# A recurrent attention layer with two expert layers on one core: group 1's triangular inverse computed by halves on GpSimd, and three changes of order

## The chip, the cores and the metric

The kernel runs on one core of a Trainium2 chip. The metric is the device time of one execution in microseconds, as the median of several runs. The core has five engines that work at the same time, each with a queue of its own that it works off in order: TensorE (PE in the rows), VectorE (DVE), ScalarE (ACT), GpSimd (POOL) and SyncE (SP), which here issues all transfers.

## The reference, cut to what matters

```python
B, H, S, D = 4, 8, 768, 48
k_n = k / (norm(k) + 1e-6)
for t in range(S):                       # per batch and head: a state of 48 x 48
    y[t] = q[t] @ state
    v_old = state.T @ k_n[t]
    state = state + beta[t] * outer(k_n[t], v[t] - v_old)
x = y as 3072 rows of 384
g = x @ w_gate                           # 384 -> 1536
x = (g * sigmoid(g) * (x @ w_val)) @ w_out       # 1536 -> 384
h = x @ w_in                             # 384 -> 2048
out = where(h > 0, h, exp(min(h, 0)) - 1) @ w_out2   # 2048 -> 384
```

All numbers are float32.

## The kernel before, in words

The 3072 tokens are cut into 12 groups of 256 (two batches, 128 time steps, all 8 heads: 16 pairs of head and batch). Inside a group the recurrence over time is computed in four chunks of 32 steps. Within a chunk the recurrence becomes a triangular system, so each group needs the inverse of a unit triangular 32 x 32 matrix for each of its 64 chunks; all of them lie side by side on the 128 partitions.

A group goes through these steps. `norms` computes the lengths of the rows of k. `prepare` transposes k and q on TensorE (L698), multiplies them with each other into small Gram matrices (L748), masks and scales these on VectorE (L758, L768), and calls `invert`. `invert` transposes the Gram matrices (L852), eliminates row by row with pairs of a product (L869, L885) and a sum (L876, L891), and transposes the result back (L900). For a group in `BLOCKED` it eliminates only the two diagonal halves of 16 rows, both in one instruction (15 pairs, `halves`), and builds the off-diagonal half by two joins on TensorE (L917, L933) with a turn (L910) and a middle step (L924) on VectorE between them and a copy on ScalarE (L937) at the end. In the kernel before that is so for group 0 alone, on VectorE; groups 1 to 11 eliminate all 32 rows on GpSimd (31 pairs, `whole`). Then `attention` applies the inverse (the X step, L994), forms the chunks' matrices (L1031, evacuated at L1050 and L1052), chains the states (L1081, L1090), reads out y (L1121) and transposes it (L1164) into the two float32r parts, high (L1174) and low (L1179), of the MoE input, in tile xa or xb.

The first MoE layer (`moe1`) runs for single groups 0 to 3 with 256 columns, and for pairs (4 and 5, and so on) with 512. Each of its 16 steps has two projections (L1350, nine matmuls each) and an output product (L1382, nine). The second layer (`moe2`) follows at the end for pairs. The first layer's weights are 24 tiles of two halves, loaded at L1228 and split by `decode` into a high and a low part: two steps on ScalarE and a copy (L1264, L1270, L1284), two steps on VectorE (L1274, L1288). All 24 stay in SBUF.

The order of the work is not that of the code. Every step is added to a planner (`Order`) with a priority, its inputs and outputs and an expected duration on its engine; `Order.run` then places the steps one after the other and so writes each engine's queue. The table `SLOW` stretches the expected durations of an inverse on GpSimd. Where the plan has TensorE idle before the first MoE matmul it puts in matmuls without use (L1551, L1557). Priorities of attention are `att_pri(g)` and a little more; group 1's preparation and attention have 14.7 (`P1`), group 2's preparation 25.

Group 1 has a tile of its own for its inverse before: `own`, which lies in the place of weight 22 (`LATE`). That weight's transfer therefore waits for group 1's X step, and group 0's second evacuation tile lies in the places of weights 21 and 23 (`LC0`). Group 1's masks are separate ones for the two Gram matrices (L758). A weight half waits for the one two before it (`PACE`). Groups 4 to 11 run the X step as two halves; groups 1 to 3 as one joint step.

Of the kernel before, what the change touches and what calls it, by code (L numbers as in the profile page):

```python
# [22 lines left out]
class Step:  # L23
    __slots__ = ("big", "shy", "alts", "pri", "succ", "np", "ready", "need", "use", "by")

    def __init__(self, alts, pri):
        self.alts = alts
        self.pri = pri
        self.succ = []
        self.np = 0  # L30
        self.ready = 0.0
        self.need = ()
        self.use = ()
        self.by = None
        self.shy = None
        self.big = False
# [15 lines left out]
class Order:  # L52
# [9 lines left out]
    SEED = 0  # L62
    SPREAD = 0.0
    FROM = 14.0
# [8 lines left out]
    def __init__(self):  # L73
        self.rng = Random(self.SEED)
# [90 lines left out]
    def link(self, b, o):  # L165
        b.succ.append(o)
        o.np += 1

    def run(self, until):
# [22 lines left out]
        while left:  # L192
# [113 lines left out]
def delta_moe_kernel(ctx: ExitStack, tc: tile.TileContext, q, k, v, beta,  # L306
# [31 lines left out]
    BIG = ()  # L338
# [324 lines left out]
    def prepare(g, p):  # L663
# [67 lines left out]
        joint = g >= 2  # L731
        if not two:
            both = [Slots([GV[x]] if g == 1 else AT, 1) for x in range(2)]
        for a in range(2):
            if not joint:
                l = []
            for par in range(2):
# [14 lines left out]
                def mask(k0, k1, a=a, par=par, h=h, w0=w0):  # L752
# [3 lines left out]
                    if g == 1 and k0 == 0 and a == 0 and par == 0:  # L756
                        buf['m1'] = TT(hm.got[0], [128, 16, 32])
                    V.tensor_tensor(out=buf['m1'][:, us].unsqueeze(2) if g == 1 and k0 == 0 else  # L758
                                    win(gr[:, a * 8 + par:a * 8 + par + 1, o:o + 1],
# [13 lines left out]
                def rest(a=a, par=par, h=h, mask=mask, masks=masks):  # L773
# [6 lines left out]
                    if g == 1:  # L780
                        one = a == 0 and par == 0
                        add(p, dvp(128, lambda: mask(0, 1)), r=[(h, a)] + zk + ([] if one else ["m1"]),
                            w=[("m1", a, par)] + (["m1"] if one else []), use=[h] if one else [h, hm],
                            need=[hm] if one else [])
                        add(p + 0.15, dvp(128, lambda: mask(1, 2)), r=[(h, a)] + zk,
                            w=[("grq", 1, a, par)] + GX[1][a], use=[h])
                        return
                    if not two:
                        add(p, dvp(256, lambda: mask(0, 2)), r=[(h, a) if g == 1 else h] + zk,
                            w=[("grm", a, par), ("grq", g % 2, a, par)] + (GX[1][a] if g == 1 else []),  # L790
                            use=[h])
                        return
# [7 lines left out]
            if not joint:  # L800
                batch(p, 6, l, g > 0, need=(both if a == 0 else []) if g == 1 else None)
                if g == 1:
                    def later_(a=a):
                        x = gr[:, a * 8:a * 8 + 8, 32 + 80 * (g % 2):64 + 80 * (g % 2)]
                        G.tensor_tensor(out=x, in0=x, in1=strict.unsqueeze(1).to_broadcast([128, 8, 32]), op=ALU.mult)
                    add(p + 0.2, pool(256, later_), r=["strict"], w=[("grq", g % 2, a, 0), ("grq", g % 2, a, 1)])
# [7 lines left out]
        invert(g, p, later, hm)  # L814
# [872 lines left out]
```

## Time and profile before

| | |
|---|---|
| median of 3 runs | 1104.2 us (1103.76 to 1109.05) |
| profiled execution, own time | 1101.52 us |
| its span, first to last instruction | 1099.8 us |
| TensorE busy | 1073.1 us, 98% of the span |
| VectorE, ScalarE, GpSimd busy | 607.1, 536.9, 347.4 us |
| mean granted TensorE clock | 0.988 of full speed |
| transfers | 57.07 MB, mean 52 GB/s |

A row of a timeline gives the start in us from the span's beginning, the duration, the engine, the line of the kernel, the operation, the tiles written and read, the number of instructions merged into the row, and in brackets how long the engine stood idle before it and whose event ended that. A row of windows gives a stretch, the busy time of an engine in it, and the clock granted to TensorE, where 1.00 is 2.4 GHz and 0.50 is 1.2 GHz.

### The profile page before, as it was taken

How to read it: one execution, taken by the hardware profiler on the slowest of the kernel's cores; microseconds unless marked ns; L12 is line 12 of the kernel's file. 1: busy time of each engine (PE TensorE's matmuls, PEld its weight loads, DVE VectorE, ACT ScalarE, POOL GpSimd, SP SyncE). 2: the span in 40 equal slices, each digit the busy share in tenths (PEclk: the TensorE clock that was granted, in tenths of full speed). 3: DMA queues.
4: the chain of work that ended last, by engine and by line, in shares of the span. 5: the costliest groups of instructions: out<-in, count | busy, mean ns of one | idle time of the engine just before them, and what ended most of it. 6: DMA issues, size and time to landing. Idle time of an engine off the chain costs nothing.

```text
span 1099.8 us, 29926 instructions
## 1 busy us (share of the span) xinstructions
PE 1073.1 (98%) x12848; PEld 931.3 (85%) x12848; DVE 607.1 (55%) x1182; ACT 536.9 (49%) x1072; POOL 347.4 (32%) x765
## 2 busy tenths in 40 slices
PE   7899899999999999999999999999999999999998
PEld 6589799999988887888777788888888888898887
DVE  7988666666345644564434466545345454444534
ACT  6878444544243424433322577645445454454443
POOL 1788787778730864064720000000000000000000
PEclk9889899999999999999999999999999999999999
DMA  8585032123002201220100456101001010000000
GB/s 168 169 216 134 17 46 46 26 39 60 2 23 43 41 2 38 42 42 16 30 13 1 153 180 205 46 1 48 10 1 58 1 58 1 10 29 1 29 2 29
DMA packets 104949, 57.07 MB, mean 52 GB/s; under 512 B 77392, under 2 KB 97360, under 8 KB 104816
## 3 DMA queue, kind: packets, MB, share of 16 engines
q1 hardware_dynamic: 104816, 55.16, 20.2%
q8 instruction: 100, 1.64, 0.6%
q14 instruction: 33, 0.27, 0.1%
HBM read 45.71 MB, written 9.44 MB: 50 GB/s over the span
## 4 chain that ended last, share of the span: by engine, by line
PE 89%; DVE 4%; POOL 3%; ACT 2%; issue 1%; DVEq 0%; POOLq 0%; ACTq 0%
PE gv L1350 26%; PE acc L1382 10%; PE gv L1476 9%; PE acc L1514 9%; PE at L1476 9%; PE at L1514 9%; PE at L1382 3%; PE at L1031 3%; PE at L1081 3%; POOL ain L869 2%; PE acc L1551 2%; PE at L994 2%; PE at L748 2%; PE at L698 1%; POOL z L876 1%
## 5 line engine op out<-in xcount | busy, mean ns | idle before, releaser
L1350 PE MATMUL gv<-xa,w 128*128 128x512 f32 (+1 forms) x1008 | 220.1, 350 | 1.6 <-DVE hb L1374 0.7
L1350 PEld LDWEIGHTS gv<-xa,w 128*128 128x128 f32 x1008 | 160.4, 190 | 27.2 <-DVE hb L1374 2.4
L1382 PE MATMUL acc<-hb,w 128*128 128x256 f32 (+1 forms) x720 | 153.8, 333 | 0.2 <-ACT hb L1369 0.2
L869 POOL TENSOR_TENSOR ain<-z,ain 128x126 f32<-128x126 f32 (+22 forms) x310 | 125.8, 406 | 57.2 <-DVE ain L852 30.6
L1350 PE MATMUL gv<-xb,w 128*128 128x256 f32 (+1 forms) x720 | 140.6, 329 | 0.0
L876 POOL TENSOR_TENSOR z<-z,ain 128x126 f32<-128x126 f32 (+22 forms) x310 | 122.5, 395 | 23.7
L1361 DVE TENSOR_TENSOR gv<-gv,tb 128x256 f32<-128x256 f32 (+1 forms) x96 | 54.1, 564 | 134.5 <-PE gv L1350 101.0
L1350 PEld LDWEIGHTS gv<-xb,w 128*128 128x128 f32 x720 | 108.6, 191 | 13.1 <-issue 0.2
L1358 ACT ACTIVATE tb<-gv 128x256 f32<-128x256 f32 (+1 forms) x96 | 47.2, 491 | 145.6 <-PE gv L1350 145.4
L1382 PEld LDWEIGHTS acc<-hb,w 128*128 128x128 f32 x720 | 106.5, 190 | 12.7 <-ACT hb L1369 0.4
L1369 ACT CAST hb<-gv 128x256 fp32r<-128x256 f32 (+1 forms) x96 | 46.0, 479 | 113.0 <-DVE gv L1361 112.6
L1491 DVE SCALAR_TENSOR_TENSOR hb<-gv,hb 128x512 f32<-128x512 f32 x45 | 31.1, 691 | 81.4 <-ACT hb L1488 81.4
L1374 DVE TENSOR_TENSOR hb<-gv,hb 128x256 fp32r<-128x256 f32 (+1 forms) x96 | 53.4, 557 | 38.1 <-PE at L1382 23.5
L1482 ACT ACTIVATE hb<-gv 128x512 f32<-128x512 f32 x45 | 26.9, 597 | 79.7 <-PE gv L1476 79.7
L1382 PE MATMUL at<-hb,w 128*128 128x512 f32 x144 | 56.2, 391 | 0.0
L1488 ACT ACTIVATE hb<-hb,zn 128x512 f32<-128x512 f32 x70 | 50.7, 725 | 2.2
L1491 DVE SCALAR_TENSOR_TENSOR hb<-at,hb 128x512 f32<-128x512 f32 x25 | 17.3, 692 | 59.0 <-ACT hb L1488 58.9
L1485 ACT ACTIVATE hb<-hb 128x512 f32<-128x512 f32 x70 | 44.3, 632 | 2.1
L1482 ACT ACTIVATE hb<-at 128x512 f32<-128x512 f32 x25 | 14.9, 597 | 61.9 <-PE at L1476 61.8
L1031 PEld LDWEIGHTS at<-gr,R 32*96 32x96 f32 x1260 | 37.0, 163 | 8.5 <-issue 5.3
L1476 PE MATMUL at<-lc,w 128*128 128x512 f32 x150 | 42.8, 393 | 0.0
L1476 PE MATMUL gv<-R,w 128*128 128x512 f32 x150 | 42.7, 395 | 0.0
(262 smaller groups left out, 2221.5 us busy)
## 6 DMA issues: line engine op xcount, KB each, us to landing
w<-in_moe_w_out_dram SPq DMA_DIRECT2D x28, 384.0 KB, 4.3
w<-in_moe_w_in_dram SPq DMA_DIRECT2D x16, 384.0 KB, 3.9
w<-in_moe_w_gate_dram SPq DMA_DIRECT2D x12, 384.0 KB, 4.2
w<-in_moe_w_val_dram SPq DMA_DIRECT2D x12, 384.0 KB, 4.2
kq<-in_q_dram SPq DMA_DIRECT2D x11, 384.0 KB, 6.4
x2d<-hb SPq DMA_DIRECT2D x16, 256.0 KB, 2.7
kp<-in_k_dram SPq DMA_DIRECT2D x10, 384.0 KB, 4.9
R<-in_v_dram SPq DMA_DIRECT2D x24, 96.0 KB, 2.2
```

The lines of the kernel that those rows point to most:

```text
L869: E.tensor_tensor(out=t, in0=z[:, l:l + 1, x:y].to_broadcast([128, m, y - x]), in1=an[:, l + 1:32, l:l + 1].to_broadcast([128, m, y - x]), ...
L876: E.tensor_tensor(out=z[:, l + 1:32, x:y], in0=z[:, l + 1:32, x:y], in1=t, op=ALU.add)
L1031: PE.matmul(bank[h[c].got[0]][0:96, i:i + 80], lhsT=R[t, u, :], rhs=gr[t, u, o0:o0 + 80], start=True, stop=True, skip_group_check=True)
L1350: PE.matmul(dst, lhsT=wt[:, a_, kk * 128:(kk + 1) * 128], rhs=X[b_][:, :, kk, :] if two else X["one", g][:, b_, kk, :], start=(n == 0), st ...
L1358: A.activation(out=c['s'], in_=gate(0), func=ACTF.Silu)
L1361: V.tensor_tensor(out=gate(1), in0=gate(1), in1=c['s'], op=ALU.mult)
L1374: V.tensor_tensor(out=c['h'][1], in0=gate(1), in1=c['h'][0].bitcast(F32), op=ALU.subtract)
L1382: PE.matmul(sums(d), lhsT=wt[:, a_, d * 128:(d + 1) * 128], rhs=c['h'][b_], start=(f == 0 and n == 0 and (two or d != 1)), stop=(f == F1 - ...
L1476: PE.matmul(x, lhsT=W[f][:, 0, a_, kk * 128:(kk + 1) * 128], rhs=x2[n][b_][:, kk, :], start=(m == 0), stop=(m == 3 * KD - 1))
L1488: A.activation(out=c['r'], in_=c['r'], func=ACTF.Identity, bias=neg1, scale=1.0)
L1491: V.scalar_tensor_tensor(out=c['r'], in0=bank[h.got[0]], scalar=0.0, in1=c['r'], op0=ALU.max, op1=ALU.add)
L1514: PE.matmul(o, lhsT=c['h'][:, b_, t * 128:(t + 1) * 128], rhs=W[f][:, 1][:, a_, :], start=(f == 0 and m == 0), stop=(f == F2 - 1 and m == 2))
```

## The change

Group 1 joins group 0 in `BLOCKED`, but its fifteen pairs run on GpSimd; the joins on TensorE follow as in group 0. It now uses the common tiles `ain` and `z` in place of `own`, so weight 22 waits for no X step and group 0's second evacuation tile lies in the places of weights 22 and 23. Group 1's four Gram products form one step with joint masks (L768). The preparation of group 2 gets priority 14.5, ahead of group 1's attention (14.7), and its k and q are loaded after weight 3 rather than 7. From weight 10 on a half waits for the one four before it. The X step of groups 4 to 11 becomes joint (`XSHY`), with gv0 among its banks. `SLOW` for group 2 rises from 1.1 to 1.4.

```diff
-    BLOCKED = (0,)
-    SLOW = (1.0, 1.5, 1.1)
+    BLOCKED = (0, 1)
+    SLOW = (1.0, 1.5, 1.4, 1.1)
...
-    PACE = 2
+    CALM = 10
+    P1 = 14.7
+    PREP = {1: P1, 2: 14.5}
+    K2 = 3
     WARM = 8
-    P1 = 14.7
-    LATE = NW - 2
-    LC0 = (NW - 3, NW - 1)
     PAIRS = 4
     THREE = 1
-    XSHY = False
+    XSHY = True
     XDVE = (0,)
-    K2 = 7
...
-        joint = g >= 2
+        joint = g >= 1
...
-    def tri(g):
-        return buf['own'][:, 0:1024] if g == 1 else ain
...
-    def invert(g, p, later, hm):
-        own = g == 1
...
+    def invert(g, p, later):
         blocked = g in BLOCKED
-        E = V if blocked else G
+        E = V if g == 0 else G
...
             def mul():
-                z = buf[Z]
-                V.tensor_tensor(out=t, in0=win(z[:, l:l + 1, 0:1], [[264, 2], [0, m], [1, e]]),
+                z = buf['z']
+                E.tensor_tensor(out=t, in0=win(z[:, l:l + 1, 0:1], [[264, 2], [0, m], [1, e]]),
...
-            on = (lambda n, f, m: lag(dve(n, f, m))) if blocked else (lambda n, f, m: [("POOL", SLOW[min(g, 2)] * (215 + 1.8 * n), SLOW[min(g, 2)] * (215 + 1.8 * n) + 80, 0, f)])
+            on = (lambda n, f, m: lag(dve(n, f, m))) if g == 0 else (lambda n, f, m: [("POOL", SLOW[min(g, 3)] * (215 + 1.8 * n), SLOW[min(g, 3)] * (215 + 1.8 * n) + 80, 0, f)])
...
-            lk = [["lc"], [f"w{x}" for x in LC0]]
+            lk = [["lc"], [f"w{NW - 2}", f"w{NW - 1}"]]
...
-            if g == 1:
-                od.link(x, sent[LATE])
...
-        norms(g, att_pri(g) - 5 if g > 1 else P1)
+        norms(g, PREP.get(g, att_pri(g) - 5))
...
-        load_w(n, src1(n), 1 + n, [] if n < AHEAD else [mark[PAUSE]], PACE)
+        load_w(n, src1(n), 1 + n, [] if n < AHEAD else [mark[PAUSE]], 2 if n < CALM else 4)
...
-            prepare(g, att_pri(g) - 5 if g > 1 else P1)
+            prepare(g, PREP.get(g, att_pri(g) - 5))
```

What is left out of the diff removes the code of `own`, of the separate masks of group 1, and settings of the planner that had no effect (a random spread of 0, an empty list of steps with a reservation). Lines of the changed kernel are some 54 lower than those of the kernel before (L1350 becomes L1296, L1382 L1328, L917 L865, L933 L881, L994 L942, L698 L684, L748 L734).

The changed code also changes the order of the queues. Three places:

TensorE, from the last chain product of group 0 to the first MoE matmuls. Names: at and gv are PSUM banks, xa is group 0's MoE input, y its attention output, w_ are weights, kp and kq hold k and q. Before:

```order
L1081 MATMUL at_87<-sv,w_23_767 48x48
L1164 MATMUL at_86<-ident,y_33_1032 128x128 x3
L1551 MATMUL acc<-tb_64 128x512 x5
L1350 MATMUL gv_84<-xa_999,w_14_593 128x256 x18
L1350 MATMUL gv_83<-xa_999,w_16_601 128x256 x18
L698 MATMUL at_88<-ident,kp 128x128 x4
L698 MATMUL at_89<-ident,kp 128x128 x4
L1382 MATMUL acc<-hb_37_1102,w_20_717 128x256 x9
L1350 MATMUL gv_84<-xa_999,w_25_826 128x256 x9
```

After (the last product of the same chain is the first row):

```order
L1027 MATMUL at_89<-sv,w_21_745 48x48
L865 MATMUL at_87<-ain,gr 32x32 x32
L1110 MATMUL at_88<-ident,y_30_1054 128x128 x3
L865 MATMUL at_86<-ain,gr 32x32 x32
L1296 MATMUL gv_83<-xa_956,w_13_514 128x256 x18
L734 MATMUL at_89<-kq 32x64 x16
L1296 MATMUL gv_84<-xa_956,w_14_553 128x256 x18
L1328 MATMUL acc<-hb_36_1237,w_18_694 128x256 x9
L1296 MATMUL gv_83<-xa_956,w_22_803 128x256 x9
```

In place of five matmuls without use stand the two first joins of group 1 (L865), with the transposes of group 0's y between them; group 2's transposes of k (L698 before) are no longer behind the first projections, and its Gram products (L734) are.

VectorE, up to the second half of group 0's MoE input (the second row that writes xa). Before:

```order
L1090 TENSOR_TENSOR st<-at_86,sv 48x4x48 x2
L1288 TENSOR_TENSOR w_28_958<-xb_112,w_28_958 128x2x384
L1179 TENSOR_TENSOR xa_999<-at_88,xa_999 128x3x128
L1274 SCALAR_TENSOR_TENSOR dt_111<-dt_111,w_21_721 128x768
L1274 SCALAR_TENSOR_TENSOR xb_112<-xb_112,w_24_797 128x768
L1288 TENSOR_TENSOR w_31_1016<-dt_111,w_31_1016 128x2x384
L1288 TENSOR_TENSOR w_32_1020<-xb_112,w_32_1020 128x2x384
L1090 TENSOR_TENSOR st<-at_87,sv 48x4x48 x2
L843 COPY z_640<-zn 128x2x16
L1274 SCALAR_TENSOR_TENSOR dt_111<-dt_111,w_26_887 128x768
L1179 TENSOR_TENSOR xa_999<-at_86,xa_999 128x3x128
```

After:

```order
L1125 TENSOR_TENSOR xa_956<-at_86,xa_956 128x3x128
L1234 TENSOR_TENSOR w_22_803<-dt_111,w_22_803 128x2x384
L1220 SCALAR_TENSOR_TENSOR xb_112<-xb_112,w_15_628 128x768
L1220 SCALAR_TENSOR_TENSOR dt_111<-dt_111,w_19_698 128x768
L848 STREAM_TRANSPOSE ain<-z_630 128x32x16
L1036 TENSOR_TENSOR st<-at_86,sv 48x4x48 x2
L1036 TENSOR_TENSOR st<-at_89,sv 48x4x48 x2
L858 STREAM_TRANSPOSE ain<-ain 128x256
L872 SCALAR_TENSOR_TENSOR z_1130<-at_87,zn,eye 128x256
L858 STREAM_TRANSPOSE ain<-ain 128x256
L1125 TENSOR_TENSOR xa_956<-at_88,xa_956 128x3x128
```

Between the first and the second half of xa stood decode steps (L1274, L1288) and an update of the state. Now group 1's transposition of the inverse (L848), its turns (L858) and a middle step (L872) stand there.

TensorE, around group 2's X step (L994 before, L942 after). xb is group 1's MoE input. Before:

```order
L1382 MATMUL acc<-hb_79_2034,w_78_2005 128x256 x9
L1382 MATMUL acc<-hb_82_2092,w_78_2005 128x256 x9
L748 MATMUL at_88<-kq 32x64 x16
L748 MATMUL at_86<-kq 32x64 x16
L1350 MATMUL gv_84<-xb_2060,w_14_593 128x256 x18
L994 MATMUL at_89<-gr,ain 32x80 x4
L994 MATMUL at_87<-gr,ain 32x80 x4
```

After:

```order
L1296 MATMUL gv_83<-xb_2146,w_13_514 128x256 x9
L734 MATMUL at_87<-kq 32x64 x16
L734 MATMUL at_88<-kq 32x64 x16
L1328 MATMUL acc<-hb_82_2176,w_74_1951 128x256 x9
L1296 MATMUL gv_83<-xb_2146,w_13_514 128x256 x9
L1296 MATMUL gv_84<-xb_2146,w_14_553 128x256 x18
L1328 MATMUL acc<-hb_86_2302,w_18_694 128x256 x9
L942 MATMUL at_86<-gr,ain 32x80 x4
L942 MATMUL at_89<-gr,ain 32x80 x4
```

One projection step of 18 matmuls stood between group 3's Gram products and the X step of group 2. Now the rest of that step, an output product, another projection step of 18 and an output product stand there.

## Rows read from the trace of the kernel before

**Rows 1.** Windows of PE by stage: start:end, length, busy (instructions), granted clock, DMA share, GB/s

```profile
60.10:123.70 63.60, 62.40 (x1153) 0.99 0.53 136
123.70:131.90 8.20, 3.10 (x129) 0.69 0.01 3
131.90:1080.00 948.10, 945.45 (x10332) 1.00 0.15 39
```

**Rows 2.** PE's timeline, 119 to 136 us: start, duration, line, operation, tiles, count, idle before

```profile
121.31 2.42 PE L1350 MATMUL gv<-xb,w 128*128 128x256 f32 x18
127.27 1.36 PE L994 MATMUL at<-gr,ain 32*32 32x80 f32 x64 [3.53 <-DVE ain L900]
130.09 1.89 PE L994 MATMUL at<-gr,ain 32*32 32x80 f32 x64 [1.46 <-DVE gr L768]
131.91 3.18 PE L1350 MATMUL gv<-xb,w 128*128 128x256 f32 x18
```

**Rows 3.** Windows of PE behind that wait, columns as in rows 1

```profile
130.00:132.00 2.00, 1.80 (x65) 0.50 0.03 8
132.00:134.00 2.00, 2.00 (x11) 0.58 0.00 0
```

**Rows 4.** GpSimd's timeline, 33 to 127 us: two inverses, first and last, two neighbours

```profile
34.03 0.81 POOL L869 TENSOR_TENSOR w<-w 128x31 f32<-128x31 f32 x1 [2.65 <-DVE w L852]
...
51.19 0.45 POOL L876 TENSOR_TENSOR w<-w 128x126 f32<-128x126 f32 x1
...
52.22 1.29 POOL L876 TENSOR_TENSOR w<-w 128x120 f32<-128x120 f32 x1
...
77.89 0.22 POOL L876 TENSOR_TENSOR w<-w 128x16 f32<-128x16 f32 x1
...
85.59 0.26 POOL L869 TENSOR_TENSOR ain<-z,ain 128x31 f32<-128x31 f32 x1 [1.78 <-DVE ain L852]
...
125.87 0.22 POOL L876 TENSOR_TENSOR z<-z,ain 128x16 f32<-128x16 f32 x1
```

**Rows 5.** VectorE: one window, then single rows of its timeline, 22 to 67 us

```profile
24.00:60.10 36.10, 33.03 (x64) 0.78 0.67 186
...
22.83 1.16 DVE L900 STREAM_TRANSPOSE ain<-z 128x512 f32<-128x512 f32 x1
24.02 0.45 DVE L910 STREAM_TRANSPOSE ain<-ain 128x256 f32<-128x256 f32 x1
...
49.87 0.94 DVE L1274 SCALAR_TENSOR_TENSOR xb<-xb,w 128x768 int32<-128x768 int32 x1
...
61.69 0.54 DVE L589 TENSOR_REDUCE sm<-kq 128x8 f32<-128x384 f32 x1
...
65.73 0.18 DVE L642 TENSOR_TENSOR sm<-sm,sm 128x16 f32<-128x16 f32 x1
```

**Rows 6.** PE's timeline, 25 to 74 us: a second join, and eight transposes

```profile
25.96 0.75 PE L933 MATMUL at<-z,ain 32*32 32x32 f32 x64
...
65.24 1.04 PE L698 MATMUL at<-ident,kp 128*128 128x128 f32 x8
66.03 1.32 PE L1382 MATMUL acc<-hb,w 128*128 128x256 f32 x9
```

**Rows 7.** PE's timeline: a joint X step, and one half of a paired group

```profile
79.61 1.24 PE L1350 MATMUL gv<-xa,w 128*128 128x256 f32 x9
80.85 1.60 PE L994 MATMUL at<-gr,w 32*32 32x80 f32 x128
82.38 1.33 PE L1350 MATMUL gv<-xa,w 128*128 128x256 f32 x9
...
435.55 0.91 PE L994 MATMUL at<-gr,ain 32*32 32x80 f32 x64
436.40 0.96 PE L1350 MATMUL gv<-xa,w 128*128 128x512 f32 x3
437.20 0.85 PE L1350 MATMUL gv<-xb,w 128*128 128x512 f32 x3
```

More of the change, by code (lines that the diff above doesn't have):

```diff
@@ L2 @@
 from itertools import count
-from random import Random
 import concourse.bass as bass
@@ L23 @@
 class Step:
-    __slots__ = ("big", "shy", "alts", "pri", "succ", "np", "ready", "need", "use", "by")
+    __slots__ = ("shy", "alts", "pri", "succ", "np", "ready", "need", "use", "by")
     def __init__(self, alts, pri):
@@ L35, in __init__ @@
         self.shy = None
-        self.big = False
 RESERVE = False
@@ L61 @@
     SLACK = 1000.0
-    SEED = 0
-    SPREAD = 0.0
-    FROM = 14.0
     LONG = 0.85
@@ L203, in run @@
                 if e == "PE":
-                    m = [o.pri for o in ready if o.big]
-                    if m:
+                    m = [o.pri for o in ready if o.shy is True]
+                    if m and RESERVE:
                         m = min(m)
@@ L755, in mask @@
                     o = 32 * k0 if g % 2 == 0 else 112 * k0
[L756 to L759, printed above, removed]
+                    V.tensor_tensor(out=win(gr[:, a * 8 + par:a * 8 + par + 1, o:o + 1],
                                             [[288, 4], [32 if g % 2 == 0 else 112, k1 - k0], [1, 32]]),
@@ L779, in rest @@
                         return
-                    if g == 1:
[L781 to L792, printed above, removed]
                     add(p, dvp(128, lambda: mask(0, 1)), r=[h] + zk, w=[("grm", a, par)], use=[h, hm])
@@ L800, in prepare @@
             if not joint:
[L801 to L806, printed above, removed]
+                batch(p, 6, l, False)
         if joint:
@@ L849, in first @@
                 l = slice(8 * n, 8 * n + 8)
-                an = tri(g).rearrange("p (l j) -> p l j", l=32)
-                src = (buf['m1'] if own else gr)[:, :, 8 * n:8 * n + 8].rearrange("p u i -> p i u")
+                src = gr[:, :, 8 * n:8 * n + 8].rearrange("p u i -> p i u")
                 V.transpose(out=an[:, l], in_=src.unsqueeze(2).to_broadcast([128, 8, 2, 16]))
-            add(p, [("DVE", 590.0, 650.0, 0, first)], r=[("m1", a, par) for a in range(2) for par in range(2)] + [Z] if own else GRM, w=[(AI, n)], use=[hm] if own else ())
+            add(p, [("DVE", 590.0, 650.0, 0, first)], r=GRM, w=[("ain", n)])
         for f in later[2:]:
@@ L873, in acc_ @@
             def acc_():
-                z = buf[Z]
-                for (x, y), t in zip(cuts, ts()):
+                z = buf['z']
+                for (x, y), t in zip(cuts, ts):
                     E.tensor_tensor(out=z[:, l + 1:32, x:y], in0=z[:, l + 1:32, x:y], in1=t, op=ALU.add)
@@ L972, in f @@
                     if g == 0:
-                        buf['lc', 1] = [TT(f"w{LC0[x]}", [128, 4, C, 80])[0:96] for x in range(2)]
+                        buf['lc', 1] = [TT(f"w{NW - 2 + x}", [128, 4, C, 80])[0:96] for x in range(2)]
                         return
@@ L993, in xstep @@
                                 o = 32 * ((c + 2 * n) % C)
-                                PE.matmul(bank[h[a, n].got[0]][o:o + 32, 80 * j:80 * j + 80], lhsT=zt_of(g)[t, u, :],
+                                PE.matmul(bank[h[a, n].got[0]][o:o + 32, 80 * j:80 * j + 80], lhsT=zt[t, u, :],
                                           rhs=gr[t, u, o0:o0 + 80], start=True, stop=True, skip_group_check=True)
             x = add(p, pe(720 * len(aa) + 50, xstep, 7, 128 * len(aa)),
-                    r=sum(([("ain1" if g == 1 else "ain", a), ("grk", a), ("grq", g % 2, a, 0), ("grq", g % 2, a, 1)] for a in aa), []),
+                    r=sum(([("ain", a), ("grk", a), ("grq", g % 2, a, 0), ("grq", g % 2, a, 1)] for a in aa), []),
                     w=list(h.values()), need=list(h.values()))
-            if g == 1:
-                od.link(x, sent[LATE])
             if shy:
```

50 lines of the change are left out of this document (16 added, 34 removed).

## The prediction

> **What bounds the kernel now.** I read the table of stages first (windows of TensorE, PE) [rows 1]. From 131.9 us to 1080 us PE is busy 945.45 of 948.10 us at full clock. So another engine's time counts only where PE waits for it, and after 131.9 us a change can pay only through what PE itself executes. What is left lies ahead of that: the head up to 60.10 us, where the first MoE matmul starts, and the stretch from there to 131.9 us.
>
> In PE's order of time I looked for the wait in that stretch [rows 2]. The first projection of group 1's MoE (eighteen matmuls on xb) ends at 123.73 us; then PE stands 3.53 us until VectorE's transposition L900 has handed over group 2's inverse, runs half of group 2's X step (L994), stands 1.46 us, and goes on to MoE work at 131.91 us. The next rows show the clock [rows 3]: after the wait the granted clock is 0.50, the 1.2 GHz level, and between 132 and 134 us still 0.58 on average. PE had been without work before it fell, and had been at work again when it rose.
>
> Who is late there is read from GpSimd's order of time [rows 4]. It holds two inverses one after the other: group 1's from 34.03 to 78.11 us (62 instructions on tile w), group 2's from 85.59 to 126.09 us. An instruction of 126 elements takes 0.45 us, the next one, of 120, takes 1.29 us: neighbours of one size differ threefold.
>
> **The sum, part by part.** The durations are those of the profiled execution: span 1099.8 us, its own time 1101.5 us, which is 2.7 us under the median of the three runs, 1104.2 us. I work out the difference against the profiled execution and set it on the median.
>
> 1. *The wait at group 2's X step.* Before, 123.73 to 131.91 us is 8.2 us for a step that takes 1.53 us at full clock (80.85 to 82.38 us) [rows 2, 7]: 6.7 us lost. At a clock of 0.58, 84% of the two microseconds from 132 us are at half rate [rows 3], which loses 0.8 us more: 7.5 us in all. In the new order 27 more MoE matmuls (18 projections and 9 of an output product) stand ahead of the X step; by the row of eighteen, 2.42 us [rows 2], they take up to 3.6 us, of which I take 3.4, since the row's end overlaps the next. Group 2's eight transposes of k and eight of q leave this stretch, 0.79 us for eight by the start of the next row [rows 6], 1.6 us together and 0.1 us for a switch back into MoE work. The two second joins of group 1 enter it, 0.75 us each [rows 6]. With a head that is 1.2 us later (part 3) PE comes to the X step at 123.7 + 3.4 - 1.7 + 1.5 + 1.2 = 128.1 us. If group 2's inverse keeps its place on GpSimd, the step is ready at 127.3 us, as before. So the wait goes; I leave 0.5 us of it. Bounds: all of it gone, or all of it back (rival 1). Taken: -7.0 us.
>
> 2. *Work of PE behind the first MoE matmul.* -1.7 us (transposes, which now lie in the head, where PE has spare time) and +1.5 us (second joins): -0.2 us. The two first joins lie in the head too and cost nothing in PE's time; what they cost is a wait.
>
> 3. *The head.* VectorE is busy 33.03 of the 36.10 us before 60.1 us [rows 5], so what moves in its queue moves the first MoE matmul. Ahead of the row that completes the second half of group 0's MoE input, the new order adds group 1's transposition of the inverse (1.16 us), two turns (0.45 us each) and two middle steps, taken as equally long, 3.0 us; of group 2's norms two sums (0.54 us) and fourteen small steps of some 0.2 us, 3.9 us; and it has five decode steps fewer there (10 for 15, 0.94 us each), 4.7 us [rows 5]. Net 2.2 us of work against 3.1 us that VectorE did not use. Ends: -1 us (decode steps that stood in front of the copies are gone) and +4 us (nothing absorbed, and the inverse somewhat late). I take +1.2 us, the middle of nothing and all of the net work. Cover: on GpSimd group 1's inverse has 30 instructions for 62. It starts later than before, since it must use group 0's tile and its four transposes stand behind three more decode steps in VectorE's queue: 34.0 + 3 x 0.94 + 0.4 = 37.2 us. At the pace of before (44.1 us for 62) thirty take 21.3 us and end at 58.5 us; at 0.45 us each, the price of the free one of 126 elements, they end at 51 us. VectorE reaches the step that waits for it at some 57 us: counted back from 61.3 us over the seven instructions that stand between it and the first MoE matmul's second half, about 4 us. So the wait is small as long as GpSimd keeps its pace. If that cover is gone, see rival 2.
>
>    The rows show that GpSimd is held at times [rows 4]. The Trainium skill, page "SBUF — State Buffer", section "Who interferes with whom", says that a VectorE instruction with both inputs in SBUF and a GpSimd instruction that reads SBUF exclude each other for a whole instruction, whichever starts first; that speaks against more GpSimd work beside decode steps, which are of this kind. By that rule the ten decode and addition steps of the head that fall beside the inverse would hold it at most 10 x 0.94 = 9.4 us, an estimate, so the inverse would end at 57 to 58 us, and the head term would be +2 rather than +1.2 us and the sum -6.1 us.
>
> 4. *Joint X step of groups 4 to 11.* A half takes 0.85 us (435.55 to 436.40 us), and the first MoE row behind it is 0.11 us longer than its like; the joint step takes 1.53 us and the row of nine behind it is 0.09 us longer than the one ahead [rows 7]. If each half stood alone between MoE work, eight groups would save 8 x (1.92 - 1.62) = 2.4 us. In the order the turns from attention to MoE work fall only from 117 to 112, so 8 x 0.17 + 5 x 0.11 = 1.9 us. Ends 0.5 and 2.4 us. Taken: -1.9 us.
>
> 5. *New waits between 60.1 and 128 us.* Before, PE lost 1.2 us between 60.1 and 123.7 us (62.40 of 63.60) [rows 1]. The new order adds two copies of the joined inverse on ScalarE behind decode steps, and PE's X step of group 1 waits for them. Ends 0 and +2.4 us. Taken: +1.0 us.
>
> 6. *Four weight halves in flight from weight 10 on*, and k and q of group 2 after weight 3: nothing. PE's waits in 60.1 to 123.7 us are 1.2 us in total [rows 1], whoever ended them, so an earlier weight has at most that to give.
>
> Sum: -7.0 - 0.2 + 1.2 - 1.9 + 1.0 = -6.9 us, that is 1094.6 us for a profiled execution and **1097.3 us** for the median.
>
> **Rivals.**
> *Rival 1: group 2's inverse stays the last to arrive.* The transposes that feed it (L802) stand behind decode steps in VectorE's queue, and the head is later. If it starts or runs 7 us longer, the X step waits again and PE falls to the lower clock again: +7.0 us, 1104.3 us. For it: its 40.5 us vary by what holds GpSimd [rows 4]. Against it: the transposes' place in the queue is the same to a few rows, and the PE order leaves 3.4 us more. Chance 0.20.
>
> *Rival 2, slower: the first join gates the first MoE matmul.* PE works in order, and both first joins of group 1 now stand ahead of L1296 of group 0; VectorE's transposition, which waits for GpSimd, stands ahead of the second half of the MoE input. If all thirty instructions took as long as the held one, 1.29 us [rows 4], the inverse would end at 37.2 + 38.7 = 75.9 us, and with 1.16 us, 0.45 us, a join and a copy the first MoE matmul would start near 78.5 us, 18.4 us late: -8.1 + 18.4 = +10.3 us, 1114.5 us. It decides from a first MoE matmul at 60.1 + 8.1 = 68.2 us on. Against it: in 34 to 78 us the mean was 0.71 us an instruction, not 1.29. Chance 0.10, with prices from 1107 us up. The rule of the SBUF page named above is this mechanism; the rows bear it out in part, since most instructions are not held.
>
> *Rival 3: the joint X step takes a bank of the paired MoE (gv0).* The gate projection would then wait for the copy out of that bank, 0.3 to 0.9 us in eight groups: +2.4 to +7.2 us in place of -1.9 us, about 1102 us to 1106 us. Against it: in the order an output product, some 2 us, stands behind the joint step. Chance 0.05.
>
> *Rival 4: the head is not later.* Then 1.2 us less, and with no new waits 1.0 less: 1095 us. Chance 0.05.
>
> **How the numbers follow.** The forecast's own case has 0.60 and lies between 1092 and 1102 us. A measurement of this kernel can tell some 0.5% (5.5 us) from no change, so faster begins under 1098.7 us: three quarters of the forecast's case (0.45), rival 4 (0.05) and 0.01 of rival 1 give 0.51. Same: 0.15 of the forecast's case, 0.18 of rival 1, rival 3: 0.38. Slower: rival 2 and the rest of rival 1: 0.11. The range of 8 in 10 runs from 1092 us (all terms at their good ends make 1093.1 us, and one microsecond is left for what the rows don't price) to 1106 us (rival 1 with two microseconds of a late head; beyond it lies rival 2).
>
> **What would show it.** In the changed profile: the first MoE matmul (L1296) near 61.3 us; GpSimd's group 1 inverse (L833, L839) in under 22 us; no wait over 1 us and no clock under 1 at group 2's X step near 128 us; 64 rather than 32 matmuls together in L942 of later groups. It would be wrong if the first MoE matmul came after 68 us, if the X step of group 2 waited over 5 us again, or if PE lost more than 6 us after 132 us.

## The result, and the profile after

| | before | after |
|---|---|---|
| median of 5 executions, us | 1103.76 (1101.51 to 1109.05) | 1095.47 (1093.55 to 1097.22) |
| profiled execution: own time / span, us | 1101.52 / 1099.8 | 1093.55 / 1091.4 |
| first MoE matmul, us | 60.10 | 60.87 |
| PE busy, us | 1073.14 | 1066.40 |
| wait and clock at group 2's X step | 3.53 + 1.46 us, then 0.50 | none, 1.00 |

The change is faster by 0.8%: the ratio of the times is 0.992, with a 95% interval of 0.9894 to 0.9946. The forecast was 1097.3 us. In the profiled executions the difference is -8.4 us (span), where the working gave -6.9 us.

The windows of PE by stage in the profile after; the columns are start:end, length, busy (instructions), granted clock, DMA share, GB/s. They answer to [rows 1]; the second holds the X step of group 2.

```profile
60.87:126.90 66.03, 64.38 (x1285) 0.97 0.46 134
126.90:130.00 3.10, 3.10 (x142) 1.00 0.02 5
130.00:1071.00 941.00, 938.06 (x10298) 1.00 0.16 39
```

Here PE loses 2.94 us after 130 us, and the stage with 5.1 us of idle time and a clock of 0.69 is gone. PE's timeline at group 2's X step, answering to [rows 2] (start, duration, line, operation, tiles, count, idle before):

```profile
126.91 1.24 PE L1328 MATMUL acc<-hb,w 128*128 128x256 f32 x9
128.08 1.64 PE L942 MATMUL at<-gr,ain 32*32 32x80 f32 x128
129.65 2.42 PE L1296 MATMUL gv<-xb,w 128*128 128x256 f32 x18
```

There is no idle time in brackets, and the row of eighteen takes 2.42 us, its full-clock time. In VectorE's timeline the transposition that completes the inverse

```profile
126.23 1.16 DVE L848 STREAM_TRANSPOSE ain<-z 128x512 f32<-128x512 f32 x1
```

ends at 127.39 us, 0.7 us ahead of PE. PE's timeline at the end of the head:

```profile
58.02 1.08 PE L865 MATMUL at<-ain,gr 16*32 16x32 f32 x64 [2.83 <-DVE ain L848]
59.03 0.90 PE L1110 MATMUL at<-ident,y 128*128 128x128 f32 x3
59.86 1.08 PE L865 MATMUL at<-ain,gr 16*32 16x32 f32 x64
60.87 4.00 PE L1296 MATMUL gv<-xa,w 128*128 128x256 f32 x18
```

The two first joins of group 1 (L865) stand directly ahead of the first MoE matmul, and the first of them waits 2.83 us for VectorE's transposition of the inverse. Who makes it late is read from GpSimd's and VectorE's timelines (they answer to [rows 4, 5]):

```profile
37.36 0.90 POOL L833 TENSOR_TENSOR ain<-z,ain 128x30 f32<-128x30 f32 x1 [4.65 <-DVE ain L802]
38.34 1.22 POOL L839 TENSOR_TENSOR z<-z,ain 128x30 f32<-128x30 f32 x1
...
52.06 0.24 POOL L839 TENSOR_TENSOR z<-z,ain 128x28 f32<-128x28 f32 x1
...
52.68 0.22 POOL L839 TENSOR_TENSOR z<-z,ain 128x16 f32<-128x16 f32 x1
52.85 2.33 POOL L663 TENSOR_TENSOR R<-R,far 128x384 f32<-128x384 f32 x2
```

```profile
37.19 0.96 DVE L1234 TENSOR_TENSOR w<-xb,w 128x768 fp32r<-128x768 f32 x1
...
38.46 0.94 DVE L1220 SCALAR_TENSOR_TENSOR dt<-dt,w 128x768 int32<-128x768 int32 x1
...
52.98 1.52 DVE L1234 TENSOR_TENSOR w<-dt,w 128x768 fp32r<-128x768 f32 x1
54.42 1.58 DVE L1220 SCALAR_TENSOR_TENSOR xb<-xb,w 128x768 int32<-128x768 int32 x1
55.92 0.94 DVE L1220 SCALAR_TENSOR_TENSOR dt<-dt,w 128x768 int32<-128x768 int32 x1
56.79 1.08 DVE L848 STREAM_TRANSPOSE ain<-z 128x512 f32<-128x512 f32 x1
```

GpSimd ends the inverse at 52.90 us; the transposition starts at 56.79 us, since an addition (L1234) and two decode steps (L1220) stand ahead of it in VectorE's queue. So it is VectorE that is late, not GpSimd's inverse; the last section comes back to two of these rows.

### The profile page after: what moved, and what is told of

Its sections match the earlier page's. It is cut to its first block, busy times and chain, and to the rows that moved or that the text cites. A ratio compares the mean times of both kernels' runs of the same rounds, so it can differ in the third digit from the quotient of the medians.

```text
span 1091.4 us, 30368 instructions
## 1 busy us (share of the span) xinstructions
PE 1066.4 (98%) x13089; PEld 929.5 (85%) x13089; DVE 607.1 (56%) x1179; ACT 536.3 (49%) x1075; POOL 321.2 (29%) x732
## 4 chain that ended last, share of the span: by engine, by line
PE 89%; DVE 4%; ACT 3%; issue 1%; DMA 1%; POOL 1%; DVEq 0%; SPq 0%; ACTq 0%; POOLq 0%
PE gv L1296 26%; PE acc L1328 10%; PE acc L1460 9%; PE gv L1422 9%; PE at L1422 9%; PE at L1460 9%; PE at L1027 3%; PE at L1328 3%; PE at L977 3%; PE at L734 2%; PE at L684 1%; PE at L1067 1%; PE at L942 1%; DMA w<-in_moe_w_out_dram 1%; PE at L1110 1%
## 5 line engine op out<-in xcount | busy, mean ns | idle before, releaser
L1296 PE MATMUL gv<-xa,w 128*128 128x512 f32 (+1 forms) x1008 | 220.6, 351 | 3.6 <-DVE hb L1320 1.6
L1296 PEld LDWEIGHTS gv<-xa,w 128*128 128x128 f32 x1008 | 161.4, 191 | 29.1 <-DVE hb L1320 3.7
L1328 PE MATMUL acc<-hb,w 128*128 128x256 f32 (+1 forms) x720 | 154.0, 334 | 0.0
L817 POOL TENSOR_TENSOR ain<-z,ain 128x126 f32<-128x126 f32 (+22 forms) x310 | 122.9, 397 | 70.3 <-DVE ain L802 40.7
L1296 PE MATMUL gv<-xb,w 128*128 128x256 f32 (+1 forms) x720 | 139.4, 328 | 0.3 <-DVE xb L1125 0.3
L824 POOL TENSOR_TENSOR z<-z,ain 128x126 f32<-128x126 f32 (+22 forms) x310 | 126.6, 408 | 23.8
L1296 PEld LDWEIGHTS gv<-xb,w 128*128 128x128 f32 x720 | 107.7, 190 | 13.1 <-DVE xb L1125 0.5
L1328 PEld LDWEIGHTS acc<-hb,w 128*128 128x128 f32 x720 | 106.3, 190 | 12.5
L1328 PE MATMUL at<-hb,w 128*128 128x512 f32 x144 | 56.2, 391 | 0.0
```

Source lines behind the costliest of these rows:

```text
L817: E.tensor_tensor(out=t, in0=z[:, l:l + 1, x:y].to_broadcast([128, m, y - x]), in1=an[:, l + 1:32, l:l + 1].to_broadcast([128, m, y - x]), ...
L824: E.tensor_tensor(out=z[:, l + 1:32, x:y], in0=z[:, l + 1:32, x:y], in1=t, op=ALU.add)
L1296: PE.matmul(dst, lhsT=wt[:, a_, kk * 128:(kk + 1) * 128], rhs=X[b_][:, :, kk, :] if two else X["one", g][:, b_, kk, :], start=(n == 0), st ...
L1328: PE.matmul(sums(d), lhsT=wt[:, a_, d * 128:(d + 1) * 128], rhs=c['h'][b_], start=(f == 0 and n == 0 and (two or d != 1)), stop=(f == F1 - ...
```

## The experiments

For every run I split the span at the first MoE matmul. Behind it, *idle* is the length less PE's busy time; *clock* is busy time x (1 - granted clock), summed over windows of 1 us up to 160 us and of 10 us from there on; *work* is the rest. So the four columns add up to the span of the profiled execution. The ratio is that of the executions to those of the kernel before on the same chip. The columns are those of the one execution that was profiled, which can be the fastest of its run (before, after, a_whole1, w_s2) or the slowest (w_halfx, w_pace2), so the ratio decides on the time and the columns only on where it went.

| run | median us | ratio (95%) | first MoE | idle | clock | work |
|---|---|---|---|---|---|---|
| before | 1103.8 | | 60.1 | 13.4 | 3.4 | 1022.9 |
| after | 1095.5 | 0.992 (0.9894-0.9946) | 60.9 | 9.1 | 1.8 | 1019.7 |
| a_again (after once more) | 1094.8 | 0.9913 (0.9894-0.9932) | 62.2 | 8.7 | 2.9 | 1019.3 |
| b_slow | 1095.2 | 0.9903 (0.988-0.9926) | 60.2 | 7.9 | 1.0 | 1023.1 |
| b_s13 | 1098.8 | 0.9961 (0.9949-0.9973) | 59.9 | 11.4 | 4.0 | 1021.6 |
| a_noslow | 1101.3 | 0.9966 (0.9949-0.9984) | 63.7 | 12.6 | 4.2 | 1019.6 |
| a_halfx | 1096.4 | 0.9908 (0.9884-0.9933) | 63.1 | 8.9 | 2.1 | 1020.8 |
| b_slow_jointx | 1098.0 | 0.996 (0.9944-0.9976) | 60.1 | 10.7 | 6.0 | 1020.2 |
| a_whole1 | 1092.6 | 0.9883 (0.986-0.9907) | 62.1 | 8.3 | 1.3 | 1017.4 |
| w_halfx | 1094.0 | 0.9907 (0.9889-0.9925) | 66.6 | 7.9 | 1.4 | 1019.4 |
| a_k7 | 1095.5 | 0.9945 (0.9925-0.9965) | 61.5 | 8.2 | 2.3 | 1021.3 |
| w_pace2 | 1095.3 | 0.9927 (0.9912-0.9942) | 65.2 | 8.3 | 6.0 | 1018.4 |
| w_prep25 | 1099.8 | 0.9965 (0.9947-0.9983) | 57.5 | 14.5 | 2.7 | 1022.0 |
| w_s2 | 1112.1 | 1.0071 (1.0054-1.0089) | 64.6 | 15.6 | 7.6 | 1021.1 |

The change against before, in this table: +0.8 (head) -4.3 (idle) -1.6 (clock) -3.3 (work) = -8.4 us.

### One number alone: b_slow

To the kernel before, nothing but the planner's expected pace of GpSimd:

```diff
-    SLOW = (1.0, 1.5, 1.1)
+    SLOW = (1.0, 1.5, 1.4, 1.1)
...
-            on = (lambda n, f, m: lag(dve(n, f, m))) if blocked else (lambda n, f, m: [("POOL", SLOW[min(g, 2)] * (215 + 1.8 * n), SLOW[min(g, 2)] * (215 + 1.8 * n) + 80, 0, f)])
+            on = (lambda n, f, m: lag(dve(n, f, m))) if blocked else (lambda n, f, m: [("POOL", SLOW[min(g, 3)] * (215 + 1.8 * n), SLOW[min(g, 3)] * (215 + 1.8 * n) + 80, 0, f)])
```

> The kernel before; only the planner's expected pace of GpSimd for group 2 rises from 1.1 to 1.4 (group 3 and later keep 1.1). TensorE's planned order then has 369 instead of 342 MoE matmuls ahead of group 2's X step; group 1's inverse stays whole on GpSimd, group 2's preparation and the half X steps stay. Theory T (the gain of the change is the wait at group 2's X step, and the 27 matmuls moved ahead of it remove it): TensorE reaches the step near 127 us, its wait falls from 3.5 + 1.5 us to under 1 us, the clock stays 1.00, about -6.5 us: 1097.3 us (1096 to 1099). Rival A (the wait went because group 1's inverse is done by halves and GpSimd is free earlier): group 2's inverse is as late as before, so the wait only moves, 1103 us or more. Rival B (the joint X step of groups 4 to 11 is most of the gain): 1102 to 1104 us.

Measured 1095.2 us: the whole gain of the change, without the inverse by halves, without group 2's earlier preparation and without the joint X step. PE's timeline there:

```profile
125.04 1.24 PE L1382 MATMUL acc<-hb,w 128*128 128x256 f32 x9
127.14 1.64 PE L994 MATMUL at<-gr,ain 32*32 32x80 f32 x128 [0.86 <-DVE ain L900]
128.71 2.42 PE L1350 MATMUL gv<-xb,w 128*128 128x256 f32 x18
```

The wait is 0.86 us and the clock stays up, though the step's input comes as late as before (127.1 us). Of the 7.9 us that idle and clock give back in this profile, 6.8 us lie between 118 and 136 us. The one number also moved the X steps of groups 3 and 4 behind 18 more MoE matmuls each, but after 136 us idle and clock are the same to 0.5 us. Rivals A and B fall as explanations of the gain.

### The same number taken back: a_noslow

```diff
-    SLOW = (1.0, 1.5, 1.4, 1.1)
+    SLOW = (1.0, 1.5, 1.1, 1.1)
```

> The changed kernel with the planner's expected pace of GpSimd for group 2 back at 1.1. Its order has 324 instead of 369 MoE matmuls ahead of group 2's X step, and 675 instead of 549 ahead of group 3's. Theory T: TensorE reaches group 2's X step some 45 x 0.134 = 6 us earlier, near 122 us, while the inverse is ready near 126 us: a wait of 3 to 5 us and the lower clock behind it are back, +4 to +7 us: 1099.5 to 1102.5 us. Rival A (the halves gave the gain) and rival B (the joint X step did): within 1 us of the changed kernel, 1094.5 to 1096.5 us.

Measured 1101.3 us. All else of the change is there, and most of its gain is gone (the intervals of the two ratios don't meet):

```profile
122.53 0.98 PE L1296 MATMUL gv<-xb,w 128*128 128x256 f32 x6 [0.21 <-DVE xb L1125]
128.17 2.43 PE L942 MATMUL at<-gr,ain 32*32 32x80 f32 x128 [4.66 <-DVE ain L848]
130.53 1.94 PE L1328 MATMUL acc<-hb,w 128*128 128x256 f32 x9
```

The X step waits 4.66 us and then takes 2.43 us for 1.64 us: the lower clock is back too. With b_slow this settles where most of the gain lies.

### A third of the way: b_s13

```diff
-    SLOW = (1.0, 1.5, 1.1)
+    SLOW = (1.0, 1.5, 1.3, 1.1)
```

with the index as in b_slow.

> The kernel before with the planner's pace for group 2 at 1.3: 351 MoE matmuls ahead of group 2's X step (342 before, 369 at 1.4), all later X steps where they were before, turns 117 as before. Theory T (the wait at that X step is what is paid, matmul for matmul): the first wait falls by 9 x 0.134 = 1.2 us to some 2.3 us, the lower clock behind it stays: 1.2 us under the kernel before, 1103.4 us (1101.5 to 1104.2). Rival (it is not that wait but the place of the later X steps that the value 1.4 moved): no change from before, 1104.7 us within 0.5 us.

Measured 1098.8 us, 4.5 us under the kernel before of that session (1103.35 us), where theory T said 1.2 us; the miss lies outside both expectations. The first wait did not shrink (3.56 us for 3.53 us): nine more matmuls stood ahead of the step, but PE had started on this stretch 0.65 us earlier, and the inverse was ready 0.46 us later. The second wait, of 1.46 us, is gone. VectorE's timeline of the kernel before shows why:

```profile
119.33 0.24 DVE L643 SCALAR_TENSOR_TENSOR sm<-sm,sm 128x16 f32<-128x16 f32 x1
126.12 1.09 DVE L900 STREAM_TRANSPOSE ain<-z 128x512 f32<-128x512 f32 x1 [6.55 <-POOL z L876]
127.09 0.61 DVE L641 SCALAR_TENSOR_TENSOR sm<-sm,sm 128x16 f32<-128x16 f32 x1
...
129.34 1.29 DVE L768 TENSOR_TENSOR gr<-at,nbs 128x512 f32<-128x512 f32 x2
```

and that of b_s13:

```profile
121.07 1.29 DVE L768 TENSOR_TENSOR gr<-at,nbs 128x512 f32<-128x512 f32 x2
126.58 1.08 DVE L900 STREAM_TRANSPOSE ain<-z 128x512 f32<-128x512 f32 x1 [4.22 <-POOL z L876]
```

Before, the transposition stood 6.55 us in VectorE's queue waiting for GpSimd, with group 3's norms and masks (L768) behind it; the masks read the two banks (at_88 and at_86 in the order before) that the second half of the X step writes, so that half waited for them. In b_s13 the masks stand ahead of the transposition. The wait of the second half was made by the order on VectorE. This accounts for a third of the 4.5 us; in the profile, which is 2.9 us shorter, another 1.3 us are *work* that I can't assign.

### The joint X step: a_halfx, w_halfx, b_slow_jointx

In a_halfx and w_halfx (the latter on a_whole1, below) it is taken out, in b_slow_jointx put into b_slow:

```diff
-    XSHY = True
+    XSHY = False
```

> The changed kernel with the X step of groups 4 to 11 in halves again (32 x 2 matmuls each, as before). The order up to group 3 is the same; turns from attention to MoE work on TensorE rise from 112 to 115. Theory T: +1.9 us (0.5 to 2.4): 1097.4 us (1096 to 1098). Rival B (the joint step is most of the gain): +4 us or more, 1099.5 us or more. If the extra bank gv0 costs the paired MoE a wait in the changed kernel, the time stays the same or falls: 1095.5 us or less.

> The changed kernel with group 1's inverse whole on GpSimd (1092.6 us) and the X step of groups 4 to 11 in halves. The order up to group 3's X step is the same, the turns from attention to MoE work rise from 110 to 114. Theory T (part 4 of the prediction): 8 x 0.17 + 4 x 0.11 = 1.8 us more, 1094.4 us (1093.1 to 1095.0). Rival (the joint step is worth nothing): 1092.6 us within 0.7 us.

> The kernel before with the planner's pace of 1.4 for group 2 and, in addition, the joint X step of groups 4 to 11. Order: 369 MoE matmuls ahead of group 2's X step as with the pace alone, turns from attention to MoE work on TensorE 111 instead of 120. Against the pace alone (1095.2 us). Theory T: 8 x 0.17 + 9 x 0.11 = 2.3 us less (0.5 to 2.4 by the working of the prediction): 1093 us (1092.7 to 1094.7). Rival (the joint step is worth nothing, since the bank gv0 makes the paired MoE wait as much as the turns save): 1095.2 us within 1 us, with new waits of TensorE on gv between 310 and 570 us.

In *work* the joint step is worth 1.1 to 1.4 us (a_halfx against the two executions of after), 1.9 us (w_halfx against a_whole1) and 2.9 us (b_slow_jointx against b_slow, nine turns fewer). In the medians, a_halfx and w_halfx are slower by 0.9 to 1.6 us and 1.4 us. By the ratios a_halfx is not slower at all (0.9908 against 0.992 and 0.9913), and the intervals of both overlap those of their partners. So the *work* has theory T's size, and the times don't prove a gain. In b_slow_jointx the step costs time in all, 2.8 us more than b_slow: the windows of PE at the end of the paired stage,

```profile
600.00:610.00 10.00, 7.50 (x157) 0.94 0.23 85
610.00:620.00 10.00, 9.43 (x135) 0.55 0.25 67
```

and its timeline there:

```profile
605.06 0.29 PE L1081 MATMUL at<-sv,lc 96*48 96x48 f32 x2 [0.65 <-DVE sv L1090]
605.65 0.51 PE L1081 MATMUL at<-sv,lc 96*48 96x48 f32 x13 [0.30 <-DVE sv L1090]
```

The last group's products on the state wait for VectorE step by step (0.65 and 0.30 us, repeated), and the clock falls to 0.55. By the trace the new order has more MoE matmuls ahead of the later X steps (765 for 738 in b_slow ahead of group 4's, 954 for 936 ahead of group 5's, and of 2592 in all 2169 for 2088 ahead of the last one), so that the attention ends later and less MoE work is left to stand between the last state products. This is not the rival named: the bank gv0 shows no new wait (PE idle between 300 and 560 us: 0.50 us in b_slow_jointx and in the changed kernel, 0.63 us before and in b_slow).

### Group 1's inverse whole again: a_whole1

```diff
-    BLOCKED = (0, 1)
+    BLOCKED = (0,)
```

> The changed kernel with group 1's inverse whole on GpSimd again (62 instructions instead of 30, no joins on TensorE, common tile). The order has 207 instead of 135 MoE matmuls ahead of group 1's X step and 450 instead of 369 ahead of group 2's. GpSimd starts near 37 us and needs 62 x 0.5 to 0.71 us = 31 to 44 us: ends at 68 to 81 us. Group 2's inverse starts after it, as late as before, and takes 38 to 41 us: ready near 127 us, while TensorE reaches its X step near 128 + 81 x 0.134 = 139 us less the joins. Theory T (the halves are worth nothing by themselves; only the order ahead of group 2's X step pays): 1094 to 1097.5 us, first MoE matmul earlier than 60.9 us. Rival A (the halves gave the gain): 1100 us or more, with a wait over 3 us at an X step of group 1 or 2.

Measured 1092.6 us, the fastest version, faster than both kernels' medians; against the changed kernel the intervals just overlap, but the profile has 1.9 to 2.3 us less *work*: the second joins (1.5 us) are gone, and all of group 2's Gram products lie in the head. The first MoE matmul came at 62.1 us, later and not earlier as expected, since these Gram products stand directly ahead of it:

```profile
59.45 2.71 PE L734 MATMUL at<-kq 48*32 48x64 f32 x128
62.09 2.29 PE L1296 MATMUL gv<-xa,w 128*128 128x256 f32 x9
```

So the halves show no gain here, and their order has about 2 us more *work*.

### What is left: a_k7, w_pace2, w_prep25, w_s2

a_k7 is the changed kernel with one line more, the others are a_whole1 with one line more. a_k7:

```diff
-    K2 = 3
+    K2 = 7
```

> The changed kernel with k and q of group 2 loaded after weight 7, as before, instead of after weight 3. Order: 153 instead of 135 MoE matmuls ahead of group 1's X step, 387 instead of 369 ahead of group 2's, turns 113. Theory T (part 6 of the prediction: the place of these loads costs nothing, and a later X step meets no wait): 1095.5 us within 1 us. Rival C (the early k and q fill TensorE's wait in the head with group 2's transposes and Gram products): these fall behind the first MoE matmul again, up to 1.7 us of transposes: 1096.5 to 1098 us.

The median is that of the changed kernel, as theory T said; the ratio is higher (0.9945 against 0.992 and 0.9913) with overlapping intervals. But rival C's mechanism is in the profile: sixteen of group 2's transposes (L684) stand behind the first MoE matmul again (160 there for 144), and *work* is 1.6 to 1.9 us higher. So it is the early load that lets these transposes lie in the head; whether the time gains by it these runs don't settle.

w_pace2:

```diff
-    CALM = 10
+    CALM = NW
```

> The changed kernel with group 1's inverse whole on GpSimd (1092.6 us), and at most two weight halves in flight throughout instead of four from weight 10 on. Order: 198 (207) MoE matmuls ahead of group 1's X step and 441 (450) ahead of group 2's, so no X step comes early. Theory T (the pace of the loads is worth nothing): 1092.6 us within 1 us. Rival C (the four loads in flight are part of the gain): 1094 us or more, with waits of TensorE on weights between 60 and 130 us.

Measured 1095.3 us, 2.7 us over a_whole1, and the intervals of the ratios don't meet. Theory T's "nothing" fails, and rival C is borne out in part: in the profiled execution, the slowest of the six (1099.6 us), PE waits once for a weight,

```profile
95.35 1.61 PE L1296 MATMUL gv<-xa,w 128*128 128x256 f32 x9 [1.09 <-ACT w L1230]
```

and the clock between 90 and 110 us is 0.87 and 0.79 (1.00 in a_whole1). The later head of this profiled execution (65.2 us) goes with a lower clock there (0.50 between 35 and 40 us), which the last section takes up.

w_prep25:

```diff
-    PREP = {1: P1, 2: 14.5}
+    PREP = {1: P1}
```

> The changed kernel with group 1's inverse whole on GpSimd and group 2's preparation at its common priority again, behind group 1's attention. Group 2's Gram products (128 matmuls, 2.7 us in the head of the run with the whole inverse) and its transposes then stand behind the first MoE matmul. Order: 234 (207) MoE matmuls ahead of group 1's X step, 513 (450) ahead of group 2's, 1143 (1026) ahead of group 5's. Theory T (what lies in TensorE's wait in the head is free): +2.7 us, 1095.3 us (1094.3 to 1096.3), first MoE matmul 1 to 3 us earlier. Rival (its place is worth nothing): 1092.6 us within 1 us. Second rival (the later X steps leave the last group's chain bare at the end of the paired stage, as in the run of the joint step alone): waits on the chain of states between 590 and 625 us with the lower clock behind them, 1097 us or more.

Measured 1099.8 us. The first MoE matmul comes 4.5 us earlier, more than expected; but idle rises by 6.2 us, *work* by 4.6 us and the clock's share by 1.4 us. The longest wait is at neither place expected: VectorE's row

```profile
114.72 1.01 DVE L575 TENSOR_REDUCE sm<-kq 128x8 f32<-128x384 f32 x2 [2.78 <-ACT kq L569]
...
119.70 1.12 DVE L1036 TENSOR_TENSOR st<-at,sv 48x384 f32<-48x384 f32 x2
```

waits for ScalarE with the update of the state (L1036) behind it, and PE's transposes wait for that update:

```profile
120.88 1.11 PE L684 MATMUL at<-ident,kp 128*128 128x128 f32 x4 [3.80 <-DVE st L1036]
```

This is the pattern of [rows 2] once more: a wait in VectorE's queue holds what stands behind it.

w_s2:

```diff
-    SLOW = (1.0, 1.5, 1.4, 1.1)
+    SLOW = (1.0, 1.5, 2.0, 1.1)
```

> The changed kernel with group 1's inverse whole on GpSimd and the planner's pace for group 2 at 2.0 instead of 1.4: 576 (450) MoE matmuls ahead of group 2's X step, 1089 (1026) ahead of group 5's, turns 104 (110). Theory T (group 2's X step has no wait left, so more matmuls ahead of it win nothing but the turns): 0.6 us less, 1092 us within 1 us. Rival (a later attention leaves the last group's chain bare at the end of the paired stage): 1095 us or more with waits between 590 and 625 us and the lower clock.

Measured 1112.1 us, 19.5 us over a_whole1. Theory T fails; the rival has the direction, but not the place. X steps that come too late leave the chain of states bare, here near 405 us already, where its products wait for VectorE one after the other:

```profile
405.53 0.29 PE L1027 MATMUL at<-sv,lc 96*48 96x48 f32 x2 [0.65 <-DVE sv L1036]
```

PE's windows there:

```profile
404.00:408.00 4.00, 2.37 (x67) 1.00 0.98 231
408.00:412.00 4.00, 3.20 (x94) 0.53 0.77 181
412.00:416.00 4.00, 4.00 (x115) 0.50 0.01 4
416.00:420.00 4.00, 3.38 (x14) 0.50 0.00 0
```

Of the 19.7 us between the two spans, idle has 7.3, the clock 6.2, work 3.7 and the head 2.5 us; the clock's 6.2 us and 4.2 us of the idle time lie between 300 and 590 us. So a larger number is not simply better.

a_again has no edit:

> The changed kernel once more, unaltered, beside the next three on the same chip: 1095.5 us within 1 us by every theory.

Measured 1094.8 us; this execution's head shows the scatter that the last section takes up.

## Why the prediction was right, point by point

The forecast's own case came, and the likeliest mechanism is the one that the runs show. Where a number agrees by luck, it is said. By the steps of the sum:

1. *The wait at group 2's X step, -7.0 us: right.* By windows of 1 us the stage of [rows 1] lost 5.1 us of idle time and 1.5 us to the clock, and 0.9 us more behind it: 7.5 us, all of which is gone. b_slow, which has this term without the other parts of the change, gained 7.6 us in span (-5.4 idle, -2.4 clock, +0.1 head, +0.15 work). The reading was coarse in one thing: it took 3.53 and 1.46 us as one wait for GpSimd, and the second was VectorE's queue (b_s13). PE came to the step at 128.08 us, for 128.1 us foretold, but that is luck: of the 4.4 us by which it came later than before, the head has 0.8 us (1.2 foretold), work 2.3 us (3.2), and new idle time and the lower clock 1.3 us, which the working of this arrival left out.
2. *Work behind the first MoE matmul, -0.2 us,* and 4. *joint X step, -1.9 us:* together -2.1 us, measured -3.3 and -3.6 us (after, a_again). The joint step alone measured 1.1 to 1.9 us of work in the changed kernel's order: right in size. Of the rest, -2.2 us (a_halfx against before) for -0.2 us, 0.5 us are four matmuls of 128x256 without use that the new order no longer has (0.134 us each by the row of eighteen); the prediction overlooked them. About 1.5 us of work stay unassigned: by the counts of the trace PE executes behind the first MoE matmul only these four and sixteen transposes less, and the second joins more.
3. *The head, +1.2 us:* +0.8 us in the profiled execution, +2.1 us in a_again. The inverse started at 37.36 us (37.2 foretold) and ended at 52.90 us (51 to 58.5), and VectorE came to its transposition at 56.79 us (some 57). The cover held. The page's rule of the shared port ("SBUF — State Buffer", "Who interferes with whom", in the Trainium skill) is borne out by the rows: the two instructions of 30 elements beside L1234 and L1220 took 0.90 and 1.22 us, where a free one of 28 took 0.24 us. But of the ten decode and addition steps that I let fall beside the inverse only these two did. Four sums that I had not counted (L959), which also have both inputs in SBUF, held it less: the instructions of 28, 52, 48 and 72 elements beside them took 0.59, 0.75, 0.64 and 0.67 us, their partners of the same size 0.27 to 0.32 us. So the estimate of 9.4 us was too high. Its end of 57 to 58 us does not follow from it either: at 0.45 us each it gives 37.2 + 13.5 + 9.4 = 60.1 us.
5. *New waits, +1.0 us:* idle between the first MoE matmul and the X step rose from 1.2 to 1.65 us, +0.45 us; the lower clock in this stretch costs 1.8 us for 0.9 us. +1.3 us in all: near the term, but two thirds of it is clock, and the step knew waits only.
6. *Pace and K2, 0:* not right for the pace: with two halves in flight throughout, w_pace2 waited 1.09 us for a weight, lost clock behind it, and was 2.7 us slower. The statement that an earlier weight has at most 1.2 us to give held for the wait and left out the clock. For K2 the medians agree with nothing (a_k7), but the work does not: the transposes' 1.7 us of part 2 hang on it.

The measured terms are -7.5 - 3.3 + 0.8 + 1.3 us, and 0.3 us of idle time elsewhere: -8.4 us for -6.9 us. The difference is mostly work.

*Rival 1* did not come, by a slack of only 0.7 us at the X step; a_noslow shows what it costs, some 6 us. *Rival 2* did not decide: the joins do gate the first MoE matmul, as it said, but at 60.87 us, and behind VectorE's queue rather than GpSimd. *Rival 3* is refuted by the idle time between 300 and 560 us. *Rival 4* named 1095 us, and 1095.5 us came; but its reason did not, since the head was later (0.8 and 2.1 us) and new waits were there. The time alone would not have told it from the forecast's case.

What the prediction did not see is how the gain is shared out. It gave the wait to the new order, rightly; but the parts that the change is named after stand in the sum at nearly nothing, and the runs show them there or below: the halves go with 2 us more work, the joint step gives 1 to 2 us of work, and one number of the planner gives a gain as large as that of the whole change.

## What to carry to other kernels

When a producer is late for an in-order engine, first move the consumer: twenty-seven matmuls of other work ahead of it (b_slow) gave here as much as the whole change. Then look at what stands behind each waiting instruction on its own engine, since its wait is passed on to work that was ready. Later is not free either: past the point where the wait ends, a later consumer can take cover away from the next chain (w_s2), so the place wants measuring on both sides.

## What was not expected of the hardware

**One program has two heads.** The granted clock of PE between 35 and 50 us differs between executions whose heads have the same instructions on PE. In a_whole1:

```profile
30.00:35.00 5.00, 3.98 (x197) 0.64 0.51 136
35.00:40.00 5.00, 3.82 (x64) 1.00 0.78 201
40.00:45.00 5.00, 5.00 (x120) 1.00 0.77 202
```

and in w_halfx:

```profile
30.00:35.00 5.00, 4.08 (x195) 0.50 0.86 196
35.00:40.00 5.00, 5.00 (x67) 0.50 0.53 166
40.00:45.00 5.00, 5.00 (x59) 0.50 0.70 183
```

In both, PE had been without work in part ahead of this (busy 3.74 and 3.51 of the 10 us from 20 us on, at clocks of 0.50 and 0.56). In the one the clock is at 2.4 GHz from 35 us on; in the other it stays at 1.2 GHz until after 50 us, and the first MoE matmul comes at 66.63 us and not at 62.09 us. The changed kernel does both: 1.00 from 35 us on in the first profile, 0.50 and 0.59 between 35 and 45 us in a_again, with the first MoE matmul 1.3 us later. This is likely a part of the scatter of the changed kernel's times, 4 to 6 us from the fastest to the slowest execution, and the reason why differences of 1 to 2 us are better read behind the first MoE matmul. What decides it was not tried.

**Holding goes both ways.** Right behind the inverse, GpSimd's two additions of 128x384 (L663, 2.33 us) lie beside VectorE's rows at 52.98 and 54.42 us, which take 1.52 and 1.58 us for 0.95 and 0.94 us. That is 1.2 us on the queue that the first join waits for. In a_again, the same program, the two additions end before VectorE comes to these rows, and all three are back at their price:

```profile
54.02 1.62 POOL L663 TENSOR_TENSOR R<-R,far 128x384 f32<-128x384 f32 x2
56.18 0.95 DVE L1234 TENSOR_TENSOR w<-dt,w 128x768 fp32r<-128x768 f32 x1
57.04 0.95 DVE L1220 SCALAR_TENSOR_TENSOR xb<-xb,w 128x768 int32<-128x768 int32 x1
```

So here each delays the other; the prediction had weighed only what VectorE does to GpSimd.
